# Six of eight pairs of f tiles by seven products in the middle blocks, two sums in place, one v buffer

## The chip, the cores and the metric

The kernel runs on one core of one Trainium2 chip. The metric is the device time of one execution in microseconds (us); several runs give a median. A profile of one execution shows every instruction on the core's engines: PE (TensorE matmul, with PEld for its weight loads), DVE (VectorE), ACT (ScalarE), POOL (GpSimd) and SP (SyncE, which here only starts transfers).

## What is computed

Linear attention, then a two-layer network with the ELU function between its layers. In the reference, cut to what matters:

```python
# q, k, v: (8, 8, 576, 64) float32: batch, heads, sequence, head_dim
q_s = softmax(q, axis=-1)
k_s = softmax(k, axis=2)                          # over the sequence
kv  = np.einsum('bhsd,bhse->bhde', k_s, v)
attn_out = np.einsum('bhsd,bhde->bhse', q_s, kv)
x = attn_out.transpose(0, 2, 1, 3).reshape(4608, 512)
h = x @ w_in                                      # w_in: (512, 2048)
g = np.where(h > 0, h, np.exp(np.minimum(h, 0)) - 1)
out = (g @ w_out).astype(np.float32)              # w_out: (2048, 512)
```

## The kernel before

**Blocks.** The 4608 tokens are worked on in 9 blocks of 512 tokens. For each block the first product h = x·w_in is made in eight steps `hg`, g = 0 to 7: eight matmuls of 128x128 weights by 512 columns (L619), into two PSUM banks, then an exp (L635) and a second activation (L655) on ACT and two operations on DVE (L658) that write ELU(h) into the ring GR. The second product of block j − 1 is interleaved with the `hg` of block j. Its contraction runs over 16 f tiles of 128 rows, that is, 8 pairs of f tiles; its output rows are token tiles of 128, two at a time (ts = 0, 1).

**Second product.** Blocks 0 and 1 use plain matmuls of 512 columns (L680), 16 for each token tile. From block 2 on, a pair of token tiles (A1, A2), a pair of f tiles and the two halves of the 512 output columns form a 2x2 by 2x2 block product, which is made from seven products of 256 columns instead of eight (Winograd's form of Strassen's method). It needs four sums of activations, S1 = A21 + A22, S2 = S1 − A11, S4 = A12 − S2 and S3 = A11 − A21, and four combinations of weights, T1 to T4. `combos` (L739) makes the weights once, on POOL, in instructions of 1024 elements. `sums` (L770) makes the activation sums for every pair of token tiles, on POOL, in instructions of 512 elements (four pairs of f tiles at a time): S1, S2 and S4 go to the buffer SB, S3 takes the place of A21. All four are made ahead of the pair's matmuls. In blocks 2 to 5 (`pair`) the first NSP = 4 of the 8 pairs of f tiles are done so (28 matmuls of 256 columns, L874), and the other four pairs by 16 plain matmuls of 512 columns (L880). In blocks 6 to 8 (`whole`) all eight pairs are done so, in two halves (56 matmuls, L804), with second buffers TB2 and SB2 that lie where q, k and v were loaded. ACT copies and DVE adds (L810, L894, L815, L922) bring the products together in OSB, with one scratch tile VT, and a transfer stores them.

**Attention.** It is done in 16 units n, two per batch element. For each unit q, k and v are loaded; ACT makes the exponentials (L380, L384); v is cast to bf16 in VB by POOL (L400, one instruction of 1152 elements); `kv_mm` (L503) makes k_s^T·v in 36 small bf16 matmuls of 64x64 weights by 65 columns; `m` scales it; qs is multiplied by its reciprocal sum (L423, POOL) and transposed, by PE (L447) in the first four units and by a transfer afterwards, which POOL then widens (L473); `ao` (L534) makes the attention output, which ACT copies to XT. There are two VB buffers. From unit 4 on the kv matmuls of two units stand together, 72 in a row: once alone (`kv2`), then behind the second ao of an odd unit (`ao(n + 1, 1, nxt)`).

**Order.** Operations are listed with the names that they read and write. The order on every engine is a table (`ORDER`, numbers of operations), worked out beforehand by a planner; from the names the kernel sets semaphore waits. So each engine runs its list in order, and what stands behind a waiting instruction waits too. Transfers start from SP's queue and, at the beginning, from POOL's: the chunks of w_in (L361), w_out (L370), and q, k and v of the first units (L345). The w_in chunks for g = 3 and above are started in the order g 3, 4, 6–7, 5, and PE takes g in the order 3, 4, 5, 6, 7.

Of the kernel before, what the change touches and what calls it, by code (L numbers as in the profile page):

```python
# [4 lines left out]
ALU = mybir.AluOpType  # L5
# [15 lines left out]
NSP, WHOLE = 4, 6  # L21
# [5 lines left out]
        "35 54 33 37 52 56 57 60 78 79 82 64 65 81 80 84 87 85 88 83 86 89 99 103 110 121 107 133 "  # L27
        "148 147 149 150 156 125 157 158 127 155 171 168 169 145 175 176 153 151 170 159 178 172 "
        "165 192 194 191 177 193 253 259 258 257 264 265 211 266 272 220 271 278 270 279 222 277 "
        "285 284 231 283 291 290 292 338 347 239 333 342 362 356 304 351 306 357 368 382 363 435 "  # L30
        "315 372 323 437 377 394 446 445 457 440 452 477 406 467 462 408 479 472 487 417 499 482 "
        "488 494 509 504 425 555 514 557 560 526 565 572 528 582 566 577 537 587 597 602 599 592 "
        "608 545 607 619 614 624 646 672 629 648 634 674 677 683 682 694 689 714 699 657 704 709 "
        "716 719 725 724 664 736 731 776 741 762 746 751 764 778 781 787 786 772 798 793 818 774 "
        "803 808 813 820 823 912 829 828 835 840 845 850 868 870 855 880 869 889 882 875 905 884 "
        "892 913 900 914 933 924 919 966 908 928 967 968 926 940 936 948 1010 1012 945 957 978 "
        "1022 953 973 980 987 982 990 1003 998 1011 1031 1017 1006 1026 1024 1043 1038 1034 1046 "
        "1067 1051 1070 1069 1072 1068 1073 1071 1077 1075 1081 1084 1079 1088 1095 1091 1098 "
        "1103 1107 "),
    "act": (  # L40
        "3 29 25 45 41 22 36 23 34 38 39 58 53 66 90 93 94 96 100 101 104 111 112 122 114 108 134 "
        "135 115 109 126 137 146 138 182 152 154 179 198 173 166 188 224 249 250 185 195 199 207 "
        "254 260 261 210 297 267 273 274 221 233 280 223 230 286 232 287 236 293 294 348 308 334 "
        "240 339 335 343 344 399 305 317 352 353 358 307 359 320 369 383 364 316 365 373 374 436 "
        "410 324 378 379 395 396 458 441 442 519 453 454 407 419 463 478 409 464 473 474 530 422 "
        "483 500 484 418 495 496 505 506 426 515 516 556 561 562 527 639 573 529 583 584 578 538 "
        "574 598 539 542 603 593 594 546 604 650 620 615 616 625 647 673 626 635 636 678 679 695 "
        "649 756 690 715 691 700 658 701 659 662 766 710 711 720 721 665 737 732 733 777 742 743 "
        "763 752 753 782 765 783 773 799 794 795 804 805 819 814 775 815 824 825 836 837 846 841 "
        "847 856 881 857 883 876 877 885 886 901 902 920 925 921 929 930 927 941 942 949 950 958 "  # L50
        "979 959 974 975 981 983 984 999 1000 1018 1023 1019 1027 1028 1025 1039 1040 1047 1048 "
        "1074 1076 1078 1080 1102 1110 "),
    "dve": (
        "4 2 5 6 0 7 30 31 46 47 26 27 28 42 43 44 49 50 51 59 55 61 62 63 67 91 92 95 97 98 102 "
        "105 106 113 123 124 117 118 119 128 136 140 129 130 141 142 160 161 162 174 167 201 202 "
        "225 251 252 196 197 255 226 256 262 263 212 213 214 215 216 217 268 269 275 276 298 281 "
        "299 282 288 289 295 296 309 241 242 310 243 244 336 245 246 337 345 346 354 355 400 401 "
        "360 361 366 367 375 376 438 439 325 326 411 327 447 412 380 381 328 397 329 398 330 459 "
        "443 444 468 469 455 456 520 480 465 466 521 481 475 476 489 501 485 486 531 532 510 497 "
        "498 511 507 427 508 428 429 430 431 432 558 517 518 563 564 559 640 567 641 585 579 586 "  # L60
        "588 589 575 576 600 601 595 596 605 547 606 548 609 549 550 621 551 552 651 617 652 618 "
        "630 631 627 628 675 676 637 684 638 680 681 696 757 692 693 758 705 706 702 703 717 718 "
        "767 712 713 666 722 738 667 723 668 768 726 669 670 671 734 735 744 747 748 745 779 780 "
        "754 755 784 800 785 788 796 797 809 810 806 807 821 822 816 817 826 827 830 838 839 842 "
        "848 851 849 852 890 891 858 859 878 879 887 893 888 906 907 903 904 909 934 922 923 935 "
        "931 932 937 943 944 946 951 952 947 960 954 961 988 989 976 977 991 1004 985 1005 986 "
        "1001 1002 1032 1033 1020 1021 1029 1030 1007 1044 1035 1045 1041 1052 1049 1050 1042 "
        "1063 1064 1082 1083 1066 1065 1085 1089 1090 1096 1097 1092 1099 1100 1104 1108 "),
    "gp": (
        "1 32 48 14 15 24 17 16 18 40 19 21 20 68 69 70 71 72 73 74 75 76 77 120 116 131 144 143 "  # L70
        "163 139 164 132 200 205 203 208 227 234 300 237 386 303 311 318 387 388 390 391 314 321 "
        "402 389 393 392 448 405 449 413 450 420 451 416 522 490 491 423 492 493 525 533 568 540 "
        "571 536 569 570 543 642 610 613 660 645 611 612 653 685 686 656 687 663 759 688 727 728 "
        "761 729 769 730 771 860 789 790 861 792 791 831 862 832 833 834 863 864 865 867 871 872 "
        "866 896 873 897 874 898 915 916 917 969 899 970 971 918 962 963 965 964 994 995 972 996 "
        "1013 1016 997 1059 1060 1014 1061 1015 1062 1055 1056 1057 1058 "),
    "sp": (
        "8 9 10 11 12 13 180 204 206 187 183 209 218 181 228 229 219 184 186 235 189 190 301 302 "
        "238 247 248 341 340 312 319 349 313 385 371 350 384 403 332 322 404 331 460 370 414 415 "
        "421 461 470 523 424 471 524 502 534 503 433 512 513 541 434 580 535 591 544 643 581 590 "  # L80
        "623 554 622 644 654 633 632 553 661 655 760 697 707 708 698 739 770 740 749 750 811 812 "
        "801 802 843 844 894 853 854 911 910 895 938 939 955 993 992 956 1009 1008 1037 1054 1036 "
        "1053 1086 1087 1093 1094 1101 1106 1105 1109 "),
# [179 lines left out]
class Gen:  # L263
# [12 lines left out]
    def alloc(self):  # L276
# [9 lines left out]
        self.SB = a("SB", [128, 3, NSP, 128], F32R)  # L286
        self.VT = a("VT", [128, 256], F32)
# [7 lines left out]
        assert nc.sbuf_base - rbase >= 22528  # L295
        self.TB2 = nc.alloc_sbuf_tensor_at("TB2", [128, 4, NSP, 256], F32R, offset=rbase)
        self.SB2 = nc.alloc_sbuf_tensor_at("SB2", [128, 3, NSP, 128], F32R, offset=rbase + 16384)
        self.QT = a("QT", [128, CH, 128], F16)
        self.VB = [a(f"VB{i}", [128, 2, CH, D + 1], BF16) for i in range(2)]
        at = nc.alloc_sbuf_tensor_at  # L300
        self.QS = [a("QS0", [128, CH, 128], F16), at("QS1", [128, CH, 128], F16, offset=base)]
# [49 lines left out]

    def raw(self, t, n):

        if t == "v":
            return (self.VR1, "vR1") if n in (1, 3) else (self.VR, "vR0")
        return self.RAW[n % 2][t], f"{t}R{n % 2}"

# [15 lines left out]
    def stage1(self, n, key, vconv="gp", what="qk"):  # L373
        S = self.S
        i = n % 2
        q, k, VB = self.RAW[i]["q"], self.RAW[i]["k"], self.VB[i]
# [5 lines left out]
        if "k" in what:  # L382
# [4 lines left out]
            for eng, h0, h1, x in {"gp": [("gp", 0, 2, "")], "act": [("act", 0, 2, "")],  # L387
# [7 lines left out]
                if eng == "act":  # L395
                    S.add("act", t_act(int(576 * (h1 - h0)), False), lambda e, dst=dst, src=src:
                          e.activation(dst, src, AF.Copy), key - 50, R=[vname], W=[f"VB{i}{x}"])
                else:
                    S.add(eng, 77 + 488 * (h1 - h0) if eng == "gp" else t_dve(int(576 * (h1 - h0))),
                          lambda e, dst=dst, src=src: e.tensor_copy(dst, src), key - 50,  # L400
                          R=[vname], W=[f"VB{i}{x}"])
# [91 lines left out]
    def kv_mm(self, n, ps, at=KV):  # L493
        i = n % 2
        P, ek, VB = self.PS[ps], self.ek(i), self.VB[i]
# [10 lines left out]
        return 615 if at == self.KV else 350, [f"kR{i}", f"VB{i}", f"VB{i}x", f"VB{i}y", f"VBone{i}"], mm  # L506
# [94 lines left out]
    def gnames(self, j, tp, gs):  # L601
        return [f"{x}{self.unit(j, g, tp)}" for g in gs for x in "gh"]
# [115 lines left out]
    def quarter(self, k, n, hi=0):  # L718

        z = 2 * NSP * hi + k  # L720
        return self.W2[:, z:z + 2 * NSP - 1:2, n * 256:n * 256 + 256]

    def combos(self, key, hi=0):
# [32 lines left out]

    def sums(self, j, ts, key, hi=0, eng="gp"):

        S = self.S
        (A11, A21, A12, A22), g, h = self.four(j, ts, hi)  # L760
        (S1, S2, S4), N = self.sb(j, ts, hi)
        last = self.summed.get(N[0][0], [])
# [418 lines left out]
```

## Time and profile before

| | |
|---|---|
| median of 3 runs | 296.62 us (296.58 to 296.95) |
| profiled execution | 296.28 us |
| its span, and what lies around it | 294.5 us, 1.78 us |
| granted TensorE clock | 1.00 |
| busy: PE, DVE, ACT, POOL | 283.3, 179.0, 210.2, 193.1 us |
| L619 (first product) | 576 matmuls of 512 columns |
| L680, L880 (plain second product) | 128 and 128 matmuls of 512 columns |
| L503 (kv) | 576 matmuls in 4 groups of 36 and 6 of 72 |
| L400, L423, L473 on POOL, mean of one | 1.15, 2.13, 1.15 us |

The profile is of one execution. An engine's busy time is the time in which at least one of its instructions was under way. Matmuls are pipelined, so the duration of one (393 ns for 512 columns) is longer than the time from its start to the next one's; what a matmul costs is read from start to start. In rows of the timeline the columns are start, length, engine, line, operation, output<-input, shape and number; in brackets stands the idle time before, and what ended it. The times of the runs hold a little more than the span.

### The profile page before, as it was taken

What the parts mean: (1) busy time and instruction counts of PE and PEld (TensorE: products, weight loads), DVE (VectorE), ACT (ScalarE), POOL (GpSimd) and SP (SyncE); (2) the same over time, 40 slices, a digit from 0 to 9 for tenths busy, and PEclk for the clock granted to TensorE, in tenths of its full rate; (3) what the DMA queues carried; (4) which work ended last, traced back from release to release, by engine and by line L of the source; (5) the groups of instructions that cost most, each with busy time, mean ns of one, the idle gap of its engine ahead of it and who ended that gap; (6) DMA issues with size and microseconds to landing.
All of it is one profiled execution on the core that took longest, in us unless ns stands there. A gap on an engine that the chain in (4) does not pass through costs nothing.

```text
span 294.5 us, 5191 instructions
## 1 busy us (share of the span) xinstructions
PE 283.3 (96%) x2082; PEld 240.4 (82%) x2082; DVE 179.0 (61%) x327; ACT 210.2 (71%) x249; POOL 193.1 (66%) x155
## 2 busy tenths in 40 slices
PE   2998999999999999999999999999999999999994
PEld 0486777788888888888888888888889899998994
DVE  2857655777545766577547656754645464465783
ACT  5867749989898969969877698766653667566510
POOL 1991347435499991966757646768578958668860
PEclk9999999999999999999999999999999999999999
DMA  7999998999974876167595925220301032020315
GB/s 260 395 371 385 388 391 267 305 231 331 315 184 141 216 242 198 40 198 215 180 214 160 267 89 114 51 62 0 71 2 36 0 90 55 19 54 2 76 33 143
DMA packets 36472, 50.01 MB, mean 170 GB/s; under 512 B 16352, under 2 KB 18144, under 8 KB 36448
## 3 DMA queue, kind: packets, MB, share of 16 engines
q1 hardware_dynamic: 29760, 34.09, 41.5%
q0 software_dynamic: 6528, 15.47, 17.4%
q8 instruction: 16, 0.26, 0.4%
q10 hardware_dynamic: 160, 0.13, 0.2%
q14 instruction: 8, 0.07, 0.1%
HBM read 36.70 MB, written 9.44 MB: 157 GB/s over the span
## 4 chain that ended last, share of the span: by engine, by line
PE 85%; DMA 5%; ACT 4%; POOL 3%; DVE 1%; POOLq 1%; issue 0%; SPq 0%
PE PS L619 41%; PE PS L804 11%; PE PS L880 10%; PE PS L874 9%; PE PS L680 9%; DMA W<-in_moe_w_in_dram 3%; PE PS L534 3%; DMA QR<-in_q_dram 2%; PE PS L503 2%; POOL W L361 1%; POOL SB L770 1%; ACT ESB L655 1%; ACT QR L380 1%; ACT ESB L635 1%; POOLq L271 1%; POOL VB L400 1%
## 5 line engine op out<-in xcount | busy, mean ns | idle before, releaser
L619 PE MATMUL PS<-XT,W 128*128 128x512 f32 x576 | 143.0, 393 | 0.9 <-DMA W<-in_moe_w_in_dram 0.9
L619 PEld LDWEIGHTS PS<-XT,W 128*128 128x128 f32 x576 | 105.3, 188 | 22.7 <-DMA W<-in_moe_w_in_dram 1.3
L658 DVE SCALAR_TENSOR_TENSOR GR<-PS,ESB 128x512 fp32r<-128x512 f32 (+1 forms) x124 | 87.2, 705 | 55.5 <-ACT ESB L655 53.4
L635 ACT ACTIVATE ESB<-PS 128x1024 f32<-128x1024 f32 x72 | 73.8, 1027 | 48.7 <-PE PS L619 48.2
L655 ACT ACTIVATE ESB<-ESB 128x1024 f32<-128x1024 f32 x64 | 68.0, 1062 | 1.5
L423 POOL TENSOR_TENSOR QS<-QR,RZQ 128x1152 f16<-128x1152 f32 (+1 forms) x16 | 30.9, 1934 | 38.9 <-DVE RZQ L415 38.8
L770 POOL TENSOR_TENSOR SB<-GR 128x512 fp32r<-128x512 f32 x18 | 23.3, 1296 | 23.4 <-DVE GR L658 10.5
L880 PE MATMUL PS<-W,GR 128*128 128x512 f32 x128 | 32.9, 393 | 0.0
L680 PE MATMUL PS<-W,GR 128*128 128x512 f32 x128 | 32.0, 393 | 0.0
L680 PEld LDWEIGHTS PS<-W,GR 128*128 128x128 f32 x128 | 23.6, 188 | 4.6
L880 PEld LDWEIGHTS PS<-W,GR 128*128 128x128 f32 x128 | 22.8, 189 | 3.8
L412 DVE TENSOR_REDUCE ZQ<-QR 128x18 f32<-128x1152 f32 (+2 forms) x18 | 21.8, 1211 | 5.8 <-ACT QR L410 4.5
L770 POOL TENSOR_TENSOR GR<-GR 128x512 fp32r<-128x512 f32 x19 | 24.7, 1301 | 0.0
L568 ACT ACTIVATE XT<-PS 128x512 fp32r<-128x512 f32 (+6 forms) x32 | 19.2, 604 | 7.3 <-PE PS L534 4.7
L770 POOL TENSOR_TENSOR SB<-SB,GR 128x512 fp32r<-128x512 f32 x18 | 23.8, 1320 | 0.9
L770 POOL TENSOR_TENSOR SB<-GR,SB 128x512 fp32r<-128x512 f32 x18 | 23.7, 1315 | 0.9 <-PE PS L880 0.4
L400 POOL CAST VB<-VR 128x1152 bf16<-128x1152 f32 (+1 forms) x16 | 17.7, 1109 | 7.7 <-DMA VR<-in_v_dram 7.7
L473 POOL CAST qsT<-QT 128x1152 fp32r<-128x1152 f16 x10 | 11.5, 1148 | 16.5 <-PE PS L534 9.5
L894 DVE TENSOR_TENSOR OSB<-OSB,PS 128x256 f32<-128x256 f32 x32 | 13.3, 415 | 12.8 <-PE PS L880 5.3
L384 ACT ACTIVATE KR<-KR 128x1152 bf16<-128x1152 f32 x16 | 18.2, 1158 | 0.2 <-DMA KR<-in_k_dram 0.2
L810 DVE TENSOR_TENSOR OSB<-OSB,PS 128x256 f32<-128x256 f32 x23 | 9.5, 418 | 12.5 <-PE PS L804 10.6
L380 ACT ACTIVATE QR<-QR 128x1152 f32<-128x1152 f32 x14 | 16.3, 1162 | 0.0
(80 smaller groups left out, 337.2 us busy)
## 6 DMA issues: line engine op xcount, KB each, us to landing
out_dram<-OSB SPq DMA_DIRECT2D x60, 128.0 KB, 2.4
QR<-in_q_dram SPq DMA_DIRECT2D x12, 576.0 KB, 5.0
KR<-in_k_dram SPq DMA_DIRECT2D x12, 576.0 KB, 5.4
VR<-in_v_dram SPq DMA_DIRECT2D x12, 576.0 KB, 5.5
W<-in_moe_w_out_dram POOLq DMA_DIRECT2D x4, 1024.0 KB, 16.9
QR<-in_q_dram POOLq DMA_DIRECT2D x4, 576.0 KB, 10.2
KR<-in_k_dram POOLq DMA_DIRECT2D x4, 576.0 KB, 10.7
VR<-in_v_dram POOLq DMA_DIRECT2D x4, 576.0 KB, 13.3
```

The lines of the kernel that those rows point to most:

```text
L400: lambda e, dst=dst, src=src: e.tensor_copy(dst, src), key - 50,
L412: S.add("dve", t_dve(m), lambda e, qp=qp, zp=zp: e.tensor_reduce(zp, qp, AX.X, ALU.add), key - 3, R=[f"qR{i}{x}" for x in xs], W=[f"ZQ{i}{ ...
L423: lambda e, qp=q[:, :, a:b, :], rz=rz, dst=qs[:, :, a:b, :]: e.tensor_tensor(dst, qp, rz, ALU.mult),
L619: last = e.matmul(P[:, t * 512:(t + 1) * 512], self.W1[:, kc, tt * 128:(tt + 1) * 128], self.XT[:, kc, rc:rc + BLK], start=(kc == 0), stop ...
L635: S.add("act", t_act(1024, True), lambda e: e.activation(esb[:, :], self.PS[ps][:, :], AF.Exp), key, W=[f"E{i}"], X=banks)
L655: S.add("act", t_act(1024, False), lambda e: e.activation(esb[:, :], esb[:, :], AF.Relu, bias=1.0, scale=-1.0), key, X=[f"E{i}"])
L658: S.add("dve", t_dve(512 if j else 1024), lambda e, u=u: e.scalar_tensor_tensor(*(x[:, :, u, :] if j else x for x in (gt, P)), 0.0, ev[:, ...
L680: last = e.matmul(dst, self.tile(jb, jj, ts), self.W2[:, jj, c0:c1], start=(jj == 0), stop=(jj == 15))
L770: lambda e, dst=dst, a=a, b=b, op=op: e.tensor_tensor(dst, a, b, op), key, R=R, W=W, X=X,
L804: last = e.matmul(dst, a[:, z, :], b[:, z, :], start=start and z == 0, stop=stop and z == NSP - 1, skip_group_check=True)
L874: last = e.matmul(dst, a[:, z, :], b[:, z, :], start=start and z == 0, stop=stop and z == NSP - 1, skip_group_check=True)
L880: last = e.matmul(self.bank((b0, b1)[p]), self.tile(j, jj, 2 * ts + p), self.W2[:, jj, :], start=False, stop=jj == 15, skip_group_check=True)
```

## The change

- `GROUPS = ((0, 4), (4, 6), (6, 8))` takes the place of the two halves: in blocks 2 to 5 the first two groups (six of the eight pairs of f tiles) go by seven products, in blocks 6 to 8 all three. `NSP` is 6. A pair of token tiles in a middle block has 42 matmuls of 256 columns (L845 in the new file) and 8 of 512 (L858). One function, `pair`, serves all blocks.
- `sums` now makes S1 (in SB) and S3 (in place of A21) ahead. The new function `late` makes S2 in place of A11 after A11·B11 has been read, and S4 in place of A12 after A12·B21. A group of two pairs of f tiles has instructions of 256 elements.
- SB keeps only S1; VT goes; TB grows to six pairs. One of the two VB buffers moves into TB's space, and serves units 1 and 3 only. So from unit 4 on there is one VB, and kv groups are done one unit at a time: `kv(4)`, `kv(5)`, then one behind each ao of an odd unit.
- XR is made twice (XL + H1 for either output row) in place of VT, and in the last pair XL is finished before XR.
- The order table is solved anew. The w_in chunks are started in the order g 3, 5, 4, 6–7, and PE takes g in the order 3, 4, 5, 7, 6; q of unit 3 is loaded ahead of k and v of unit 2.

```diff
-NSP, WHOLE = 4, 6
+GROUPS, WHOLE = ((0, 4), (4, 6), (6, 8)), 6
+NSP = 6
...
-        self.SB = a("SB", [128, 3, NSP, 128], F32R)
-        self.VT = a("VT", [128, 256], F32)
+        self.SB = a("SB", [128, NSP, 128], F32R)
...
-        self.TB2 = nc.alloc_sbuf_tensor_at("TB2", [128, 4, NSP, 256], F32R, offset=rbase)
-        self.SB2 = nc.alloc_sbuf_tensor_at("SB2", [128, 3, NSP, 128], F32R, offset=rbase + 16384)
+        self.TB2 = nc.alloc_sbuf_tensor_at("TB2", [128, 4, 2, 256], F32R, offset=rbase)
+        self.SB2 = nc.alloc_sbuf_tensor_at("SB2", [128, 2, 128], F32R, offset=rbase + 8192)
...
-        self.VB = [a(f"VB{i}", [128, 2, CH, D + 1], BF16) for i in range(2)]
+        self.VB = [a("VB0", [128, 2, CH, D + 1], BF16),
+                   at("VB1", [128, 2, CH, D + 1], BF16, offset=tbase + 8192)]
...
+    @staticmethod
+    def vb(n):
+        return 1 if n in (1, 3) else 0
...
+    def sums(self, j, ts, key, grps):
+        for grp in grps:
+            (A11, A21, A12, A22), (m, h, n, g) = self.four(j, ts, grp)
+            S1, N = self.sb(j, ts, grp)
+            own = [f"T1{grp}"] if grp == 2 and (j, ts) != (NBLK - 1, 1) else []
+            one = self.add_sum(grp, S1, A21, A22, ALU.add, key, h + g + own, N, [], self.summed.get(N[0], []))
+            self.third[j, ts, grp] = self.add_sum(grp, A21, A11, A21, ALU.subtract, key, m, [], h, [one])
+
+    def late(self, j, ts, key, grps):
+        for grp in grps:
+            (A11, A21, A12, A22), (m, h, n, g) = self.four(j, ts, grp)
+            S1, N = self.sb(j, ts, grp)
+            self.summed[N[0]] = [self.add_sum(grp, A11, S1, A11, ALU.subtract, key, N, [], m,
+                                              [self.third[j, ts, grp]])]
+            self.add_sum(grp, A12, A12, A11, ALU.subtract, key, m, [], n, [],
+                         "dve" if (j, ts) == (NBLK - 1, 1) else "gp")
...
         def first():
+            mms(0, H[0], A11, B11, m, None, True)
+            copy(XL, H[0], [f"O{x}L"], b0)
+            mms(1, H[3], S1, T1, N1, 3, True)
+            mms(0, H[0], A12, B21, n, None)
+            self.late(j, ts, key, grps)
 
         def second():
+            if not full:
+                std(0, 2 * NSP, 16, False)
...
+        def third():
             copy(YL, H[0], [f"O{y}L"] + over, b0)
+            mms(1, H[1], A11, T2, m, 0)
+            dve(XR, XL, H[1], [f"O{x}L"], [f"O{x}R"], [f"b{b1}"])
+            dve(XR, XR, H[3], [], [], [f"O{x}R", f"b{b1}"])
+            mms(0, H[2], A12, B22, n, None, stop=True)
             done.append(dve(YR, XR, H[2], [f"O{x}R"], [f"O{y}R"] + over, [f"b{b0}"]))
             self.store(j, 2 * ts, Y[:, :512], y, key)
+            mms(1, H[1], A21, T3, h, 1)
+            dve(XR, XL, H[1], [f"O{x}L"], [f"O{x}R"], [f"b{b1}"], done)
 
         def fourth():
+            if not full:
+                std(1, 2 * NSP, 16, False)
+            elif not end:
+                dve(XR, XR, H[3], [], [], [f"O{x}R", f"b{b1}"])
+            mms(1, H[1], A22, T4, g, 2, stop=True)
             dve(XL, XL, H[1], [], [], [f"O{x}L", f"b{b1}"])
             if end:
                 self.store(j, 2 * ts + 1, X, x, key, 0, 256)
+            if not full or end:
+                dve(XR, XR, H[3], [], [], [f"O{x}R", f"b{b1}"])
...
-            yield from (ao(n, 0), ao(n, 1), first(n + 1, "q"), loads(("q", n + 3)), wide(n + 1),
-                        ao(n + 1, 0))
-            nxt = (n + 2, n + 3) if n + 2 < NU else ()
-            for m in nxt:
-                yield from (first(m, "k"), loads(("v", m + 1)))
-            yield from (ao(n + 1, 1, nxt), loads(("k", n + 4), ("k", n + 5)))
+            yield from (ao(n, 0), ao(n, 1), first(n + 1, "q"), loads(("q", n + 3)), wide(n + 1))
+            more = n + 2 < NU
+            if more:
+                yield from (first(n + 2, "k"), loads(("v", n + 3)))
+            yield ao(n + 1, 0, (n + 2,) if more else ())
+            if more:
+                yield from (first(n + 3, "k"), loads(("v", n + 4)))
+            yield from (ao(n + 1, 1, (n + 3,) if more else ()), loads(("k", n + 4), ("k", n + 5)))
```

## The prediction

> **What bounds the kernel now.** I read the page first: engine totals, the forty slices, the chain that ended last.
>
> ```profile
> PE 283.3 (96%) x2082; PEld 240.4 (82%) x2082; DVE 179.0 (61%) x327; ACT 210.2 (71%) x249; POOL 193.1 (66%) x155
> PEclk9999999999999999999999999999999999999999
> PE 85%; DMA 5%; ACT 4%; POOL 3%; DVE 1%; POOLq 1%; issue 0%; SPq 0%
> ```
>
> PE is busy nearly always, at full granted clock, and is 85% of the chain. POOL, which gets most of the new work, has a third of the span free. Next the PE timeline, for the real cost of a matmul: the busy durations overlap, so I take start-to-start times.
>
> ```profile
> 101.92 0.64 PE L874 MATMUL PS<-TB,GR 128*128 128x256 f32 x4
> 102.40 0.64 PE L874 MATMUL PS<-W,GR 128*128 128x256 f32 x4
> 102.88 0.64 PE L874 MATMUL PS<-W,SB 128*128 128x256 f32 x4
> 103.36 2.00 PE L880 MATMUL PS<-W,GR 128*128 128x512 f32 x8
> 105.20 0.39 PE L619 MATMUL PS<-XT,W 128*128 128x512 f32 x1
> ...
> 38.13 0.48 PE L503 MATMUL PS<-VB,KR 64*64 64x65 bf16 x36
> 38.55 0.96 PE L680 MATMUL PS<-W,GR 128*128 128x512 f32 x3
> ...
> 58.97 0.78 PE L503 MATMUL PS<-VB,KR 64*64 64x65 bf16 x72
> 59.68 1.21 PE L619 MATMUL PS<-XT,W 128*128 128x512 f32 x4
> ```
>
> Twelve 256-column matmuls take 103.36 − 101.92 = 1.44 us, 0.120 each; eight of 512 columns take 105.20 − 103.36 = 1.84, 0.230 each (0.2285 over 16 or more). A kv group of 36 takes 38.55 − 38.13 = 0.42 us from its start to the next start, one of 72 takes 59.68 − 58.97 = 0.71: 36 more matmuls cost 0.29, so 0.13 belongs to the change over and back. The single starts around both add 0.09 (first kv late) and 0.10 to 0.12 (the matmul after the next). So each kv group costs 0.31 to 0.32 us on top of its matmuls.
>
> Third the groups by form on POOL, and the table by stage (columns: window, its length, then PE, PEld, DVE, ACT and POOL busy).
>
> ```profile
> L770 POOL TENSOR_TENSOR SB<-GR x18: 1287/1296/1303, 89.1 to 278.6; 128x512 fp32r<-128x512 f32 x18
> L739 POOL TENSOR_TENSOR TB<-W x4: 2405/2406/2410, 73.0 to 199.8; 128x1024 fp32r<-128x1024 f32 x4
> 129.00:159.50 30.50, 30.50 (x257) 26.59 (x243) 19.94 (x43) 25.20 (x31) 21.57 (x17) 1.00 0.65 171
> ```
>
> A middle block is 30.5 us of PE without a gap; POOL fills about 70% of it. Last the two ends, from the timeline and the chain.
>
> ```profile
> 24.78 3.97 PE L619 MATMUL PS<-XT,W 128*128 128x512 f32 x16 [0.86 <-DMA W<-in_moe_w_in_dram]
> ...
> 283.57 0.71 PE L804 MATMUL PS<-W,SB 128*128 128x256 f32 x4 [0.25 <-POOL SB L770]
> ...
> 289.57 1.23 PE PS L804 x8
> 290.82 0.42 DVE OSB L810
> ```
>
> By single starts, PE stands 1.02 us before 24.78 (a chunk of w_in), 0.34 around 53.3 (ACT), 0.49 around 283.57 (POOL) and 0.27 around 289.57 (DVE). Between 54 and 283 us there is no stall over 0.12 us, so there an instruction added to PE is paid in full.
>
> **Matmuls of blocks 2 to 5.** Eight pairs of token tiles go from 28 matmuls of 256 columns and 16 of 512 to 42 and 8; the order of PE's instructions shows it done, so that the change might not do what it says is no rival here. Per pair: 8 × 0.2285 − 14 × 0.1195 = 0.155 us. With 0.227 and 0.120 it is 0.136, with 0.230 and 0.1185 it is 0.181. Eight pairs: −1.09 to −1.45, taken −1.24. The Trainium skill, TensorE: Matmul & The Clock Gate, section Back-to-back issue gap, gives an isolated warm gap of N/2.4 + 2.5 ns; by it the saving would be an estimated 0.198 per pair, 1.58 in all. The trace's 0.2285 and 0.1195 differ from its 0.216 and 0.109, and the measurement decides.
>
> **kv groups.** VT goes, TB grows, VB1 moves into TB's space, so from unit 4 on there is one v buffer, and units 4 to 15 can no longer be done two at a time. Six groups of 72 become twelve of 36, as the order of PE shows. The matmuls stay 432; six more changes over and back cost 6 × 0.31 = +1.86 us. They stand in blocks 1 to 7, where PE has no gap to hide them, which excludes a gain or a zero. The ends are 6 × 0.28 = 1.7 and 6 × 0.33 = 2.0.
>
> With one buffer a v cast (L400, 1.15 us on POOL) must wait for the kv group before and end before the next. In the closest place PE has 2.06 us of other matmuls between the two groups, which covers 1.15 and the two handovers with 0.7 to spare. Queued behind that cast on POOL are qs multiplies (2.13 us) and sums; with the cover gone PE would stand for the cast's rest, at most 1.15 a time.
>
> **Sums on POOL.** Per pair there were four of 512 elements; now four of 512 and four of 256. A 256 sum is not in the trace. A line through 1.30 (512) and 2.41 (1024) gives 0.75; the bounds are 0.65 (half of 1.30) and 1.30 (no cheaper). I take 0.75. A middle block gets 8 × 0.75 = 6 us more: POOL goes from 21.6 to about 27 of 30.5 in the fullest block (in others from 19 to 25). Over the kernel 133 sums instead of 76: about 55 × 1.30 + 78 × 0.75 = 130 us instead of 99, so POOL near 224 us. On PE this costs nothing while POOL keeps up.
>
> S2 and S4 now overwrite A11 and A12, so each waits for PE's last reading of that part (A11·B11, A12·B21), and PE's later products wait for them. Behind a late sum on POOL stand the next block's sums, widens (1.15) and casts; for those wait PE's kv and ao. Between A11·B11 and the product with S2 the order of PE has 3.5 us or more of other matmuls, against 1.30 + 0.75 and two handovers; the tightest place, with what POOL has queued ahead by its order at the rows' durations, leaves about 0.6. I add nothing, and put the failure of this cover under the rivals. ACT and DVE keep their two copies and six adds per pair; in place of VT, XR is made twice.
>
> **Start.** The chunk for g5 is now loaded before those for g4 and g6–g7, and PE takes g7 before g6. PE reaches the last chunk's first matmul at about 25.7, when it landed at 24.73 in the trace: the 1.02 stall falls to 0.1 or 0.2. But PE then soon meets data: v of unit 2 lands at 36.2 if it follows q3 (34.7 before), and v of unit 3 landed at 44.66, with its cast ending at 46.0 and its kv group at 46.27 in the trace. A later POOL cast in front of unit 3's transposes would cost some 0.7. Bounds −1.1 and +0.7; near the row at 46.27, which no reordering of w_in moves, I take −0.3.
>
> **End.** After the last hidden product ends, 124 matmuls remain instead of 120; those four are only moved. Now nine or ten POOL sums of 0.75 and one or two of 1.30 follow the last GR (278.54), about 10 us, until 288.5; the trace's POOL sums took 1.74 and 1.62 there beside a DVE sum of 1.67. PE stalled 0.76 here before; a chain worked through by these rows gives 0.5 to 1.1. And one more 0.42 us add follows the last matmul: XL, then XR. Bounds −0.34 (no stalls) and +0.9; taken +0.6.
>
> **Sum**, against the profiled execution's 296.28 (span 294.5 and 1.78 around it): −1.24 + 1.86 − 0.3 + 0.6 = +0.9, 297.2. The median of the runs lies 0.34 above that execution, so I forecast **297.5**.
>
> **Rivals.** *The stalls go* (other side). The solved order takes away what PE still stands for: 1.02 at the start, 0.34 near 53.3, 0.76 at the end. For it: all are waits set by order. Against: the loads behind the start do not move, and the extra add does not either. With all 2.1 gone the profiled time is 296.28 + 0.62 − 2.1 + 0.42 = 295.2, the median 295.5; it decides once 1.6 of the 2.1 is gone. Chance 0.2.
>
> *They cancel.* The start keeps its whole 1.0 and the end is as before plus the add, or the start keeps 0.3 and the end loses its stalls: +0.04 or so, 296.6 in the median; within ±0.6 (0.2%, about what a measurement of this kernel tells from no change). Chance 0.2.
>
> *POOL becomes the bound.* If a 256 sum costs near 1.30, POOL has 21.6 + 10.4 = 32 us in a block of 30.5, and every late sum is waited for: 1.5 us in each of the two or three fullest blocks, 3 to 4.5 in all, 300.5 to 302. The first 0.7 lost in front of a kv group would show it. For it: sums now stand in line with PE both before and after. Against: 2.41 for twice the elements shows little fixed cost. Chance 0.13.
>
> *Small matmuls dearer.* If 256 columns cost more than 8/14 of 512, the swap itself loses; at 0.145 each it would be +1.6 instead of −1.24, hence 300.3. The trace has 0.1195 over whole groups of them. Chance 0.02. The same section of the skill gives sustained spacings of 81 ns at 128 columns and 131 at 512, by which the swap would lose; this trace's spacings do not agree with it.
>
> **How the numbers follow.** My case has 0.45, from 297.0 to 298.9; with the rivals, slower gets 0.45 + 0.13 + 0.02 = 0.60, same 0.2, faster 0.2. The range 295.6 to 299.6 takes in cancelling, the upper half of the faster case and the beginning of the POOL case, and leaves out about 0.2. In my case alone the unknown costs (−1.45 to −1.09, 1.7 to 2.0, the start and the end) rarely all fall on one side.
>
> **What would show it.** In the new profile: 2130 matmuls; twelve kv groups of 36 at 0.42, each with its late starts; 256 sums at 0.75; POOL at 224 us; no wait of PE for POOL over 0.2 us between 54 and 275; the stall of 1.0 at 24 us gone but given back by 54; two adds after the last matmul. Wrong I would be if middle blocks show PE waits, or if PE enters block 2 over 0.8 us earlier than before.

## The result, and the profile after

| | before | changed |
|---|---|---|
| median of 20 runs each | 296.62 us (296.16 to 296.98) | 297.12 us (296.82 to 298.45) |
| profiled execution | 296.28 us | 297.21 us |
| its span | 294.5 us | 295.4 us |
| busy PE, POOL | 283.3, 193.1 us | 284.8, 221.1 us |

The changed kernel is slower: its time is 1.0020 of the time before, 95% interval 1.0013 to 1.0027. The medians lie 0.50 us apart, the two profiled executions 0.93. The forecast was 297.5 us, in the range 295.6 to 299.6, with 0.6 for slower.

The page first: engine totals, the granted clock, the chain.

```profile
PE 284.8 (96%) x2129; PEld 242.6 (82%) x2129; DVE 176.8 (60%) x326; ACT 210.9 (71%) x249; POOL 221.1 (75%) x216
PEclk9999999999999999999999999999999999999999
PE 91%; POOL 2%; ACT 2%; DVE 1%; DMA 1%; issue 0%; POOLq 0%
```

PE is still the bound, and more of the chain than before (91% against 85%). POOL has 28 us more work and is not on the chain except at the end. Next the PE timeline, at one of the kv groups behind unit 5.

```profile
69.81 0.51 PE L551 MATMUL PS<-qsT,MBLK 128*128 128x384 f32 x2
70.25 0.48 PE L520 MATMUL PS<-VB,KR 64*64 64x65 bf16 x36
70.67 0.72 PE L697 MATMUL PS<-W,GR 128*128 128x512 f32 x2
```

A group of 36 takes 0.42 us to the next start, as forecast, and there are twelve. By the start times of the single matmuls, the late starts around kv groups between 54 and 276 us come to 1.93 us in 18 places before (six groups) and to 3.78 us in 36 places now (twelve): 0.315 us a group, 1.85 us more. No other late start in that stretch is over 0.04 us in the changed kernel.

Then POOL: the group of S1, both forms together (duration lowest, median, highest), and the table by stage (window, its length, then busy PE, PEld, DVE, ACT and POOL).

```profile
L797 POOL TENSOR_TENSOR SB<-GR x31: 729/745/1321, 88.4 to 278.3; 128x256 fp32r<-128x256 f32 x18, 128x512 fp32r<-128x512 f32 x13
...
98.40:129.00 30.60, 30.60 (x242) 26.70 (x241) 20.07 (x38) 26.36 (x32) 29.52 (x26) 1.00 0.54 157
129.00:159.50 30.50, 30.50 (x279) 26.73 (x278) 19.34 (x40) 23.37 (x30) 27.44 (x26) 1.00 0.77 210
```

The median in the first row, 745 ns, is that of both sizes taken together; the 18 sums of 256 alone have a median of 0.742 us, where 0.75 was worked out. POOL is busy 27.4 us of the window that held 21.6 before, and 29.5 of 30.6 in the fullest one; still PE has no gap in either. Last the two ends: the PE timeline at the start, the chain at the end, and SP's queue at the end (start, time taken by the issues, number).

```profile
22.12 6.74 PE L636 MATMUL PS<-XT,W 128*128 128x512 f32 x29
...
286.49 4.38 PE PS L845 x34
290.88 0.02 issue
290.90 0.43 DVE OSB L866
291.33 0.02 issue
291.36 0.42 DVE OSB L866
...
289.16 1.89 SPq L730 DMA_DIRECT2D out_dram<-ESB  x2
291.09 2.52 SPq L730 DMA_DIRECT2D out_dram<-OSB  x4
```

The wait of 1.02 us for a w_in chunk is gone: 29 matmuls of the first product run through. At the end two adds follow the last product, and SP starts four transfers behind each other from 291.09 to 293.61, the last of them 1.31 us later than in the kernel before, whose row is this.

```profile
289.58 2.72 SPq L713 DMA_DIRECT2D out_dram<-OSB  x4
```

There the last of four is started at 291.70 and the span ends at 294.48; now at 293.01 and 295.41. From the start of PE's last matmul to the end of the span it is 3.99 us before and 4.83 now. (ESB is a buffer of the first product that also holds one of the last two output tiles before it is stored.) The second add ends at 291.78, 1.23 us ahead of SP's last start; before, the last add ended at 291.24, 0.46 us ahead of it.

### The profile page after: what moved, and what is told of

It is laid out like the page before. It is cut to its first block, busy times and chain, and to the rows that moved or that the text cites. A ratio compares the mean times of both kernels' runs of the same rounds, so it can differ in the third digit from the quotient of the medians.

```text
span 295.4 us, 5358 instructions
## 1 busy us (share of the span) xinstructions
PE 284.8 (96%) x2129; PEld 242.6 (82%) x2129; DVE 176.8 (60%) x326; ACT 210.9 (71%) x249; POOL 221.1 (75%) x216
## 4 chain that ended last, share of the span: by engine, by line
PE 91%; POOL 2%; ACT 2%; DVE 1%; DMA 1%; issue 0%; POOLq 0%
PE PS L636 44%; PE PS L845 24%; PE PS L697 9%; PE PS L858 5%; PE PS L551 3%; PE PS L520 2%; POOL GR L797 2%; PE PS L948 2%; DMA QR<-in_q_dram 1%; PE PS L464 1%; DVE GR L675 1%; DVE OSB L866 1%; PE PS L563 0%; ACT qsT L471 0%; ACT ESB L672 0%
## 5 line engine op out<-in xcount | busy, mean ns | idle before, releaser
L797 POOL TENSOR_TENSOR GR<-GR 128x512 fp32r<-128x512 f32 (+1 forms) x65 | 62.9, 980 | 5.1 <-PE PS L845 3.9
L866 DVE TENSOR_TENSOR OSB<-OSB,PS 128x256 f32<-128x256 f32 x83 | 34.5, 416 | 35.2 <-PE PS L845 34.5
L845 PE MATMUL PS<-W,GR 128*128 128x256 f32 x288 | 46.0, 284 | 0.3 <-POOL GR L797 0.3
L845 PE MATMUL PS<-TB,GR 128*128 128x256 f32 x288 | 43.5, 283 | 0.0
L845 PEld LDWEIGHTS PS<-W,GR 128*128 128x128 f32 x288 | 40.7, 191 | 2.5 <-POOL GR L797 0.5
L845 PEld LDWEIGHTS PS<-TB,GR 128*128 128x128 f32 x288 | 39.7, 190 | 1.7
L797 POOL TENSOR_TENSOR SB<-GR 128x256 fp32r<-128x256 f32 (+1 forms) x31 | 30.1, 975 | 13.5 <-DVE GR L675 11.8
L697 PE MATMUL PS<-W,GR 128*128 128x512 f32 x128 | 33.1, 398 | 0.0
L797 POOL TENSOR_TENSOR GR<-SB,GR 128x256 fp32r<-128x256 f32 (+1 forms) x31 | 29.9, 980 | 2.7 <-PE PS L845 2.2
L697 PEld LDWEIGHTS PS<-W,GR 128*128 128x128 f32 x128 | 23.2, 188 | 4.9 <-DMA W<-in_moe_w_out_dram 0.3
L858 PE MATMUL PS<-W,GR 128*128 128x512 f32 x64 | 17.6, 396 | 0.0
L871 ACT ACTIVATE OSB<-PS 128x256 f32<-128x256 f32 x27 | 10.1, 380 | 9.8 <-PE PS L845 7.5
```

The costliest lines, as they stand in the source:

```text
L697: last = e.matmul(dst, self.tile(jb, jj, ts), self.W2[:, jj, c0:c1], start=(jj == 0), stop=(jj == 15))
L797: lambda e: e.tensor_tensor(dst, a, b, op), key, R=R, W=W, X=X, after=after)
L845: last = e.matmul(dst, a[i][:, y_, :], b[i][:, y_, :], start=start and i == 0 and y_ == 0, stop=stop and i == len(grps) - 1 and y_ == z - ...
L858: last = e.matmul(self.bank(bk), self.tile(j, jj, 2 * ts + p), self.W2[:, jj, :], start=False, stop=stop and jj == jj1 - 1, skip_group_che ...
L866: S.add("dve", t_dve(256), lambda e: e.tensor_tensor(dst, a, b, ALU.add), key, R=R, W=W, X=X, after=after)
```

## The experiments

Ratios are against the kernel before, timed on the same chip, with 95% intervals. "Idle" below means: the start time of a matmul less the spacing (0.229 for 512 columns, 0.119 for 256, and so on) of all matmuls ahead of it.

**The kv groups apart, in the kernel before.**

```diff
                 parts = [self.ao_mm(n, x, ps)] + [self.kv_mm(m, ps, y) for m, y in cols]
+                if len(parts) == 3:
+                    parts = [parts[1], parts[0], parts[2]]
```

> The kernel before, with one edit: in five of its six double kv groups the two matmuls of ao stand between the two units' kv matmuls instead of ahead of them. No work is added. Theory (each change from fp32 matmuls to the 64x64 bf16 ones and back costs PE 0.31 us, and nothing hides it): five more of them, +1.55 us, so about 298.2 us, ratio 1.0052; groups of 36 take 0.42 us from start to next start. Rival (the changed kernel lost its time elsewhere, to the order or to POOL, and kv groups cost what their matmuls cost): 296.6, ratio 1.000.

Measured: 298.50 us, ratio 1.0045 (1.0027 to 1.0063). The timeline of PE at one of the five places:

```profile
97.29 0.48 PE L503 MATMUL PS<-VB,KR 64*64 64x65 bf16 x36
97.70 0.50 PE L534 MATMUL PS<-qsT,MBLK 128*128 128x256 f32 x2
98.14 0.48 PE L503 MATMUL PS<-VB,KR 64*64 64x65 bf16 x36
98.55 0.73 PE L874 MATMUL PS<-TB,SB 128*128 128x256 f32 x4
```

Without a single matmul more, the kernel is 1.3 us slower by the ratio and 1.7 by the medians; the late starts around kv groups after 54 us grow from 1.93 to 3.77 us, 0.37 for each of the five groups, where 0.31 was expected. The rival is out: the change over and back is what costs. Two ao matmuls between two groups do not hide it; from 97.70 to 98.14 they take 0.44 us, 0.24 of which is their own spacing.

**Four pairs instead of six, in the changed kernel.**

```diff
     def groups(self, j):
-        return (0, 1, 2) if j >= WHOLE else (0, 1)
+        return (0, 1, 2) if j >= WHOLE else (0,)
...
-                std(0, 2 * NSP, 16, False)
+                std(0, 8, 16, False)
```

> The changed kernel, but with four instead of six pairs of f tiles by seven products in blocks 2 to 5: the other eight tiles go by plain matmuls again, and the 32 sums of 256 elements go from POOL (24 us). The weights of the two pairs stay combined in place, so the output differs from the reference's. Theory (the swap saves PE 0.16 us a pair and the sums on POOL cost nothing): 1.3 us slower than the changed kernel, 298.4 us, 1.006 of the kernel before. Rival (the late sums in place make PE wait, so part of the swap's saving is lost to POOL): between 297.1 and 298.0, 1.0015 to 1.0045.

Measured: 300.58 us, ratio 1.0120 (1.0097 to 1.0143); both expectations missed. The work of PE, number by spacing, is 1.31 us more than in the changed kernel, as it should be. The rest is waiting: between 54 and 275 us PE is idle 6.6 us, against 4.0. Its largest wait, in the chain:

```profile
106.81 1.04 ACT ESB L647
107.84 0.02 issue
107.86 1.07 ACT ESB L667
108.94 0.02 issue
108.96 0.70 DVE GR L670
109.66 0.02 issue
109.69 0.70 DVE GR L670
110.39 0.04 issue
110.43 2.14 PE PS L631 x8
```

PE reaches the first product of the next g before ACT and DVE have emptied its PSUM banks, probably because the order was solved for a PE that does other matmuls ahead of them. So the run bears out the swap by number and spacing of its matmuls, but not by its time, and it says nothing on POOL: of 2.3 us of late starts between 54 and 276 us that lie apart from kv groups, 2.0 stand at the first product.

**The w_in chunk of g5 first, in the kernel before.**

```diff
-        "1 32 48 14 15 24 17 16 18 40 19 21 20 ...
+        "1 32 48 14 15 24 17 16 18 40 19 20 21 ...
```

> The kernel before, with one edit: the w_in chunk for g5 is started ahead of that for g6 and g7. Theory (the stall of 1.02 us at 24.8 us goes, but later loads and casts take half of it back by 54 us, as in the changed kernel): 296.1 us, ratio 0.998 to 0.9985. Rival one (all is taken back by the v load that lands near 44.7): 296.6, ratio 1.000. Rival two (nothing is taken back): 295.6, ratio 0.9965.

Measured: 296.40 us, ratio 0.9982 (0.9971 to 0.9994). The wait at 24.8 us falls from 1.02 to 0.26, and at 54 us PE stands 0.3 us better in the profiled execution (idle 8.76 against 9.08). By the ratio about half is given back, as the theory had it, though the interval is wide (0.2 to 0.9 us kept). The profiled execution does not show the gain: its span is 294.6 us against 294.5, as PE waits 0.4 us for DVE at 59.73, behind the kv group, where it did not wait before.

**XR ahead of the last product, in the changed kernel.**

```diff
-            elif not end:
+            else:
                 dve(XR, XR, H[3], [], [], [f"O{x}R", f"b{b1}"])
+            if end:
+                self.store(j, 2 * ts + 1, X, x, key, 256, 512)
             mms(1, H[1], A22, T4, g, 2, stop=True)
```

> The changed kernel, but in the last pair of token tiles XR is finished and stored before the last product, as in the kernel before, instead of after XL. Theory (the end is 0.85 us longer by one add of 0.42 and by four transfers started behind it): 0.5 to 0.7 us faster than the changed kernel, since PE waits 0.2 to 0.3 for that add again; about 296.5 us, ratio 0.999 to 1.000. Rival (PE's wait ahead of the last product takes the add's place in full): 297.1, ratio 1.0015 to 1.002.

Measured: 297.56 us, ratio 1.0019 (1.0001 to 1.0037), so nothing gained. The chain at the end:

```profile
289.76 0.02 issue
289.78 0.76 DVE OSB L866 x2
290.55 0.04 issue
290.59 1.23 PE PS L845 x8
291.82 0.02 issue
291.84 0.42 DVE OSB L866
```

PE waits 1.0 us at 290.59 for XR's second add, which on DVE stood behind XL of the other pair, and XL waits for a product. The next run put that right.

> As the run with XR finished ahead of the last product, but XR's second add stands on DVE right behind its first, ahead of the other pair's XL, which waits for a later product. Theory (the 1.0 us wait of PE in that run came from XR standing behind XL of the other pair on DVE; then the end's add and its transfers do come ahead of the last product): PE waits 0.1 to 0.3, and the kernel is 0.5 to 0.7 us faster than the changed one, 296.5 us, 0.999 to 1.000 of the kernel before. Rival (the two adds between the products take as long wherever they stand): 297.1, 1.0015 to 1.002.

Measured: 297.69 us, ratio 1.0035 (1.0020 to 1.0050). PE's wait falls to 0.39 us as expected, and still nothing is gained: SP's issue of the second ESB transfer takes 1.42 us there (1.38 in the changed kernel, 0.60 before), and the four starts behind it run from 292.05 to 294.77. So it is not the add that ends last, but the queue behind it. That led to the run on ACT's queue below.

**More work for POOL, in the changed kernel.** The second of the two runs has only `j < WHOLE` as its condition.

```diff
             one = self.add_sum(grp, S1, A21, A22, ALU.add, key, h + g + own, N, [], self.summed.get(N[0], []))
+            if grp == 1 and j < WHOLE:
+                one = self.add_sum(grp, S1, A21, A22, ALU.add, key, h + g, N, [], [one])
```

> The changed kernel, with one more sum of 256 elements on POOL for each pair of token tiles in blocks 2 to 5 (S1 of the second group is made twice): 8 x 0.75 = 6.0 us more POOL work, 1.5 us a block. Theory (POOL has room in every middle block, 0.6 us at the tightest place): 0 to 0.4 us slower than the changed kernel, 297.1 to 297.5, 1.0015 to 1.003. Rival (POOL is the bound of the middle blocks): most of the 6 us, 301 to 303, 1.015 to 1.02.

> The changed kernel, with S1 of both groups made twice in blocks 2 to 5: 8 x (1.30 + 0.75) = 16.4 us more POOL work, 4.1 us a block, which fills the fullest block (27 of 30.5 us) to the brim. Theory (POOL now meets its limit in some blocks): 1 to 5 us slower than the changed kernel, 298 to 302, 1.005 to 1.018. Rival one (POOL was the bound already): the whole 16 us, 313. Rival two (room everywhere): no change, 297.1.

Measured: 298.00 us, ratio 1.0051 (1.0033 to 1.0068), and 302.38 us, ratio 1.0201 (1.0183 to 1.0218). Against the changed kernel's 1.0020 that is about 0.9 us for 6.0 us more POOL work, and 5.4 us for 16.4. PE's idle time between 54 and 275 us: 4.0 in the changed kernel, 4.7 with the small dose, 8.9 with the large one. The waits of PE in the run with the large dose (total, times, longest):

```profile
PE PS L847 <- POOL GR L797: 2.4, 4, 1.0
```

So the first dose meets the limit in a few places and the second in more: POOL is not the bound of the changed kernel, but there is hardly any room left. The expectation of at most 0.4 us for the small dose was too low, and that of at most 5 for the large one a little.

**Two v buffers.** Room came from SB, with all four sums made in place (S3 as A22 − S2, late), and kv groups two units at a time.

```diff
-            one = self.add_sum(grp, S1, A21, A22, ALU.add, key, h + g + own, N, [], self.summed.get(N[0], []))
-            self.third[j, ts, grp] = self.add_sum(grp, A21, A11, A21, ALU.subtract, key, m, [], h, [one])
+            self.add_sum(grp, A21, A21, A22, ALU.add, key, g, [], h, [])
...
+            self.add_sum(grp, A21, A22, A11, ALU.subtract, key, m + g, [], h, [])
```

> The changed kernel, but with two v buffers again, and with them the kv matmuls of units 4 to 15 two units at a time. The room comes from SB: S1 is made in place of A21, and S3 late, as A22 - S2, in its place after S1*T1 has been read; the number of sums stays. Theory (the twelve kv groups cost six changes over and back too many, 0.31 us each, nothing else in the middle does): 1.9 us faster than the changed kernel, 295.2 us, 0.995 of the kernel before. Rival (the late sums in place are what costs, and here there are half as many again of them): 297.1 or more, ratio 1.0015 and up.

Measured: 314.00 us, ratio 1.0594 (1.0575 to 1.0613). The waits of PE:

```profile
PE PS L827 <- POOL GR L784: 8.0, 6, 5.0
PE PS L548 <- ACT qsT L489: 1.4, 1, 1.4
```

That is far from the theory's 295.2 us. The late starts around kv groups do fall, to 2.03 us between 54 and 276. But PE waits 5 us at 297.8 for a late sum of the last block, and many times from 58 us on, where loads and casts come later than in the changed kernel (the cast of v for unit 6 at 69.6 instead of 65.5), and that swamps it. The order was carried over by hand, so this is no verdict on the idea.

**Five pairs and two v buffers.**

```diff
-GROUPS, WHOLE = ((0, 4), (4, 6), (6, 8)), 6
-NSP = 6
+GROUPS, WHOLE = ((0, 4), (4, 5), (5, 8)), 6
+NSP = 5
+TWO = 8
...
-        self.VB = [a("VB0", [128, 2, CH, D + 1], BF16),
-                   at("VB1", [128, 2, CH, D + 1], BF16, offset=tbase + 8192)]
+        self.VB = [a(f"VB{i}", [128, 2, CH, D + 1], BF16) for i in range(2)]
...
-            yield ao(n + 1, 0, (n + 2,) if more else ())
+            two = n + 2 >= TWO
+            yield ao(n + 1, 0, (n + 2,) if more and not two else ())
```

> The changed kernel, but with five instead of six pairs of f tiles by seven products in blocks 2 to 5. That leaves room for a second v buffer, and the kv matmuls of units 8 to 15 stand together two units at a time again (eight kv groups after unit 3 instead of twelve). S1 and S3 stay ahead, S2 and S4 late, as in the changed kernel. Theory (four changes over and back saved, 4 x 0.31 = 1.24; half of the swap's 1.31 given up): 0.6 us faster than the changed kernel, 296.5 us, ratio 0.999 to 1.000. Rival (pairing holds back the loads and casts behind the first unit's kv matmuls, as it did in the run with two v buffers, since the order was not solved for it): slower than the changed kernel, 298 or more.

Measured: 298.51 us, ratio 1.0057 (1.0042 to 1.0071); the rival. The late starts around kv groups fall by 1.15 us (2.63 in 25 places), close to the 1.24 expected; but other waits of 1.3 us stand between 77 and 211 us, and the waits at the end grow from 0.64 to 1.83 us, where the third group's sums on POOL are now of three pairs. So in these places pairing is worth what the count says, and the order as it stands loses as much elsewhere; whether an order solved for it would keep the gain is not shown.

**Two of the last transfers from ACT's queue, in the changed kernel.**

```diff
-            q = "act" if x and c1 - c0 == 256 else "sp"
+            q = "act" if x and (c1 - c0 == 256 or (jb, ts) in ((NBLK - 1, 1), (NBLK - 1, 2))) else "sp"
```

> The changed kernel, but two of the last output transfers (the second half of the rows of the last two full tiles) are started from ACT's queue instead of SP's. Theory (SP starts six transfers one behind the other at the end, 0.64 us each, and the last starts 1.3 us later than in the kernel before): the last start comes about 0.8 us earlier, the end 0.4 to 0.7; 296.6 us, ratio 0.999 to 1.001. Rival (the end is set by the last add and its transfer alone): 0 to 0.2 us, 297.0, 1.001 to 1.002.

Measured: 296.57 us, ratio 0.9994 (0.9984 to 1.0004). The issues at the end, on SP's and ACT's queue:

```profile
289.29 0.47 SPq L730 DMA_DIRECT2D out_dram<-ESB  x1
290.48 2.41 SPq L730 DMA_DIRECT2D out_dram<-OSB  x3
...
289.29 0.55 ACTq L730 DMA_DIRECT2D out_dram<-ESB  x1
290.49 2.14 ACTq L730 DMA_DIRECT2D out_dram<-OSB  x3
```

SP's last start moves from 293.01 to 292.23, though the last matmul starts 0.13 us later, and from the start of the last matmul to the end it is 4.16 us instead of 4.83. That is the theory's 0.4 to 0.7, and half a microsecond in the medians (of separate runs): as much as the changed kernel lost against the one before, but that one has a queue at its end too, as the next run shows.

**Both gains in the kernel before.** The chunk of g5 first, and the same two transfers from ACT's queue.

> The kernel before with the chunk for g5 ahead of g6 and g7, as in the earlier run, and the same two output transfers from ACT's queue. Theory (both gains add: 0.45 at the start, and at the end 0.3 to 0.45, as its last transfer starts 0.46 us behind its add): 295.9 us, ratio 0.997. Rival (the end gains nothing): 296.25, 0.998 to 0.9985.

Measured: 295.89 us, ratio 0.9968 (0.9957 to 0.9979), as the theory had it. From the start of the last matmul to the end it is 3.39 us instead of 3.99. This is faster than both kernels. It is also 0.68 us faster by the medians than the changed kernel with the same two transfers moved, whose start already has the chunk of g5 ahead of those of g6 and g7: with both repairs in both kernels the change still loses.

## Why the prediction was right

The direction and the mechanism were right: the swap saves, the kv groups cost more than it saves, and POOL keeps up. Step by step, as differences between the two profiled executions:

| step | forecast, us | in the traces, us |
|---|---|---|
| matmul swap | −1.24 | −1.31 (112 × 0.1192 − 64 × 0.2290) |
| kv groups | +1.86 | +1.85 (late starts 3.78 − 1.93) |
| start | −0.3 | −0.57 |
| end | +0.6 | +0.73 |
| small rest | | +0.2 |
| span | +0.9 | +0.93 |

That the total agrees to 0.03 us is partly luck: the start came out 0.27 us better than forecast and the swap 0.07, the end 0.13 and the small rest 0.2 worse. The medians are only 0.50 us apart (0.4 to 0.8 by the interval of the ratio). The forecast took the runs to lie 0.34 us above the profiled execution, as they did before; the changed kernel's lie 0.09 below its own, so the table explains a pair of executions that differs by more than the kernels do, and 297.5 was 0.38 too high.

**The swap** was read off start-to-start times, and comes out within 0.1 us.

**kv groups.** The step that decided the sign held: 0.31 us a change, six more, in full. The run with the groups apart shows it without the rest of the change. The Trainium skill, TensorEngine Tiling (Array Packing), section Key Properties, says that changing the tiling mode drains TensorE; the late starts on both sides of the 64x64 groups agree with that, and 0.315 us is what these traces put on it. No run separates the change of shape from that of the type, fp32 to bf16 and back. But in the trace before, PE goes to f16 transposes of 128x128 at 44.44 us without a late start and comes back from them with 0.06 us lost, so a change of type alone cost little there. And the last of a group's three late starts, the 0.10 to 0.12 on the second matmul behind it, does not belong to kv groups alone: in the run with the large dose of POOL work the wait of 1.15 us at 110.96 is followed by one of 0.10 us on the next matmul, and so are five other waits of that run.

**Start.** The stall went and was partly given back, as argued. In the traces PE's idle time at 54 us is 9.08 before and 8.94 after, and the changed kernel issues 13 warm-up matmuls (fillers whose result the kernel does not use) where 14 ran before (0.43 us): 0.57. With the warm-ups counted as idle, the two stand within 0.1 us of each other at 24.5 us; the changed kernel is 1.2 us ahead at 26, where the stall was, and 0.57 at 54. The size is uncertain by more than it looks: in the nine executions profiled with this start the idle time at 54 us lies between 8.81 and 9.95 us, so one trace fixes it to half a microsecond at best. The run of the chunk of g5 alone gave −0.5 by its ratio and nothing in its profiled execution.

**End.** Right in size, but a step was missing. The waits went from 0.76 to 0.64 us; from the last matmul on it is 0.85 longer. The forecast put 0.42 there, for one add more, and never counted SP's queue: six transfers started one by one, with a start of 1.38 us among them. In the trace SP's last start comes 1.23 us behind the end of the second add, so it was the queue that it waited for; finishing XR ahead of the last product left the time as it was. The add and the queue do not simply add up: with two transfers on ACT's queue in either kernel the stretch is 4.16 and 3.39 us, still 0.77 apart, 0.45 of it by the end of the last add. The term was saved by its stalls, taken as 0.18 longer where they were 0.12 shorter.

**POOL.** Forecast: 0.75 a sum, 224 us, about 27 of 30.5 in the fullest block, no cost. Measured: 0.742, 221 us, no wait of PE for it between 54 and 275. Between the two closest kv groups PE has 2.31 us of other matmuls, where 2.06 was read. But the fullest window, another than the forecast took, holds 29.5 us, since weight combinations fall into it too; the dose runs show that another 1.5 us a block already costs. The chance of 0.13 for that rival was not idle.

**The rivals.** The stalls did go at the start, but of the 1.6 us that the faster case needed only 0.57 came of it there and 0.12 at the end. *They cancel* came close: the 0.50 us between the medians lies inside the ±0.6 that the prediction gave it, though the interval leaves out a difference of zero. Dearer small matmuls found no support: the changed kernel's 672 matmuls of 256 columns start 0.119 us apart.

## What to carry to other kernels

Count the changes between matmul shapes of different tiling on a saturated PE as instructions of their own, with a price read off start-to-start times; a buffer that is given up can be paid for there. When a forecast is checked term by term against one profile of each kernel, compare the differences of the medians too. At the end of a kernel, list the transfer starts of each queue like instructions: the last one may be late because of its queue and not because of its data. An edit to a kernel whose order was solved for other durations measures the order as much as the edit, unless the edit leaves the order alone.

## What the runs showed of the hardware

A transfer start on SP took 0.47 to 0.60 us in most rows at the end and 0.8 in some, but 1.38, 0.92, 1.42, 1.44, 1.19 and 1.38 us for the second ESB transfer in six profiles with the changed kernel's end (the changed kernel, both runs on its last add, two v buffers, both doses). In the runs with four and five pairs the same start took 0.60 us. In the six, the OSB transfer started last ahead of the two ESB transfers took 3.4 to 3.9 us from its start to its landing, in those two runs 2.4 us. With the second ESB transfer on ACT's queue no start took over 0.81 us in the run on the changed kernel, though that OSB transfer took 3.95 us there too. What lengthens the start was not tried.
